# Rows of logits that go through memory in the expert stages k = 2 to 7, and two products a tile for the tokens' numbers where k is odd

## The chip, the core and the metric

The kernel is one program on one core of a Trainium2 chip. The core has a matrix engine (TensorE: PE in the profile, its weight loads PEld), a vector engine (VectorE, DVE), an activation engine (ScalarE, ACT), GpSimd (POOL) and SyncE (SP); each takes its instructions in a fixed order and waits on semaphores. POOL and SP issue DMAs, POOL the indirect ones (gathers and scatters). The metric is the device time of one execution in microseconds (us), the median of several.

## The reference

Three parts follow one another, cut here to what matters:

```python
# 1. retention with decay, blocks of 64: q, k, v are (2, 8, 768, 64); x is (1536, 512)
x = attn_out.transpose(0, 2, 1, 3).reshape(1536, 512)
# 2. tokens to 8 experts, 192 tokens each, greedily by falling logit
logits = x @ w_gate
for idx in np.argsort(-logits.flatten()):
    tok, e = idx // 8, idx % 8
    if assigned[tok] >= 0 or counts[e] >= 192: continue
    assigned[tok] = e; counts[e] += 1
for e in range(8):
    out[assigned == e] = np.maximum(x[assigned == e] @ w1[e], 0) @ w2[e]   # 512 -> 1024 -> 512
# 3. a dense layer on every token: 512 -> 2048 -> 512, ELU between
g = elu(out @ w_in);  result = g @ w_out
```

## The kernel before

The retention comes first (the first 95 us), and it leaves the logits and the tokens' rows `xd` in memory. Then come eight stages k = 0 to 7. The greedy assignment is done expert by expert: the expert that fills first, its 192 tokens, then the expert that fills first among those left, and so on. `R.n` is the number of tiles of 128 tokens still listed: 12 for k = 0 and 1, 9 for k = 2 and 3, 6 for 4 and 5, 3 for 6 and 7. Before each even stage from k = 2 on `pack(k)` drops the assigned tokens: one scatter per tile from POOL (L710) into `open`, then one fetch (`new`, L723).

For a stage k the steps of routing are, in this order:

- `update(k)`. `close` (L739 to L742) shuts the filled expert and leaves each token's best open logit in `m` (128 partitions, one column per tile). `rows_` (L760) transposes on PE, for each tile, that tile's column spread over 128 columns, so that PSUM holds the 128 logits as a row on every partition; ACT copies up to four such tiles at once into `mrow` (L763). Then `cmp` compares on DVE for each tile c the whole of `mrow` with column c of `m` (L425, L421, L428), and `tally` (L783) sums the outcome on PE, n small products a tile. The result is each token's rank.
- `choose(k)`. `theta`, `close`, `mine` find the next expert to fill, its number (`EV`, read by SP for the weights' loads) and its tokens; `index` (L877) makes the 192 tokens' numbers by products of a one-hot matrix `ohs` with `mt`, one product per tile and column. One product gives 128 slots, so an even stage has two columns (slots 0 to 127 and 128 to 191), an odd stage three: slots 64 to 191, 0 to 63 on partitions 0 to 63, and 0 to 63 again on partitions 64 to 127. The third serves only `ixm`, the list by which the middle output tile of a pair of stages is sent. `gb` and `ga` (L896, L902) gather the rows of `xd` into `xb` and `xa`.
- `x_parts(k)` transposes `xb` and `xa` (L943) and splits the result into `xt`; `weights(k)` loads w1 and w2 and, for k > 1, splits them on ACT and DVE (`w1p`, `w2p`: L1011, L1014).

The stage's own work on PE is h (`xt`, `w1p`), y (`ht`, `w2p`), g (`yt`, `wih`/`wil`) and, by pairs of stages, the output products (`gg`, `woh`/`wol`). Numbers with more than 16 bits are taken as a sum of two 16-bit parts, three products each. The routing of stage k + 1 is worked in beside g of stage k and what follows it.

All steps are handed to a planner (`Plan`) as tasks with an engine, a cost, dependencies, a lag, and a bonus `ahead`; it orders them by its own costs and writes one fixed order for each engine. POOL's scatters of `pack` also wait for the PE instruction that stands ahead of them in that order. So a changed task moves others on all engines.

Of the kernel before, what the change touches and what calls it, by code (L numbers as in the profile page):

```python
# [19 lines left out]
FT = mybir.dt.float32  # L20
# [3 lines left out]
AF = mybir.ActivationFunctionType  # L24
# [14 lines left out]
AHEAD, XAHEAD, WAHEAD, EAHEAD, GLAG, APART = 15.0, 4.0, 5.0, 3.0, 3.5, 1.2  # L39
# [7 lines left out]
class Plan:  # L47
# [10 lines left out]
    def add(self, eng, cost, fn, *deps, lag=0.0, ahead=0.0, look=0.15, mode=None):  # L58


        t = dict(eng=eng, cost=cost, fn=fn, lag=lag, ahead=ahead, look=look, mode=mode, n=len(self.tasks))
        t["deps"] = [d if isinstance(d, tuple) else (d, 0.0) for d in deps if d is not None]
        self.tasks.append(t)
        return t
# [38 lines left out]
def kernel(  # L103
# [13 lines left out]
    nc = tc.nc  # L117
    B, H, S, D = q.shape
    C = 128
    NC = S // C  # L120
    NT = B * NC
# [5 lines left out]
    CAP = N // E  # L127
# [5 lines left out]
    route = ctx.enter_context(tc.tile_pool(name="route", bufs=1))  # L133
    dram = ctx.enter_context(tc.tile_pool(name="dram", bufs=1, space=bass.MemoryType.DRAM))
    psum = ctx.enter_context(tc.tile_pool(name="psum", bufs=1, space=bass.MemoryType.PSUM))

    def bank(tag, bufs=1):
        return psum.tile([128, 512], FT, name="ps_" + tag, tag=tag, bufs=bufs)
# [25 lines left out]
    identf = consts.tile([128, 128], FT)  # L164
# [31 lines left out]
    for i, (r0, o) in enumerate(((0, 0), (0, 64), (64, 0))):  # L196
# [3 lines left out]
                                  ap=[[E, step], [256 * E, HP // 2], [1, E]]))  # L200
# [60 lines left out]
    xd = dram.tile([N, DM], FT)  # L261
# [119 lines left out]
    class R:  # L381
        n = NT
# [4 lines left out]
    m = route.tile([128, NT], FT, name="m")  # L387
# [9 lines left out]
    mrow = route.tile([128, N], FT, name="mrow")  # L397
# [65 lines left out]
    add = hp.add  # L463
# [82 lines left out]
    while at < len(pairs):  # L546
        n = max(pairs[at])
# [12 lines left out]
    use, use2 = [None, None], [None, None]  # L560
# [53 lines left out]
    add = pl.add  # L614
# [14 lines left out]
    RB_ = ("m", "o")  # L629
# [36 lines left out]
    EV, ev_task = {}, {}  # L666
    wst = {}
    rk = route.tile([128, NT], FT, name="rk")
    th = route.tile([128, 2, E], FT, name="th")
    mt = route.tile([128, NT], HF, name="mt")  # L670

# [60 lines left out]
    def update(k):  # L732

        n, L, act, ws = R.n, R.L, R.act, wst[0]
        sh = [128, n, E]
        t = tp_[:, 0:n, :]

        def close():
            nc.vector.tensor_scalar(cl, e8, ws, None, op0=OP.is_equal)  # L739
            nc.vector.tensor_scalar(cl, cl, -2.0 * BIG, BIG, op0=OP.mult, op1=OP.add)  # L740
            nc.vector.tensor_tensor(L, L, cl[:, None, :].to_broadcast(sh), op=OP.min)
            nc.vector.tensor_reduce(m[:, 0:n], L, axis=AX, op=OP.max)  # L742

        def top():
            nc.vector.tensor_tensor(t, L, m[:, 0:n, None].to_broadcast(sh), op=OP.is_equal)
            nc.vector.tensor_tensor(t, t, e8b.to_broadcast(sh), op=OP.mult)
            nc.vector.tensor_reduce(wv[:, 0:n], t, axis=AX, op=OP.max)
            nc.vector.tensor_tensor(t, wv[:, 0:n, None].to_broadcast(sh), e8b.to_broadcast(sh), op=OP.is_equal)
            nc.vector.tensor_tensor(oh[:, 0:n, :], t, act[:, :, None].to_broadcast(sh), op=OP.mult)
        d = add("DVE", 0.95, close, R.task, last_compare[0])  # L750
        row = []
        for b in range(0, n, 4):
            e = min(n, b + 4)
            i, old, use = rbank.take()
            S = {}

            def rows_(b=b, e=e, i=i, S=S):
                S["p"] = p = bank(RB_[i])
                for c in range(b, e):
                    nc.tensor.transpose(p[:, (c - b) * 128:(c - b + 1) * 128], m[:, c:c + 1].to_broadcast([128, 128]), identf)  # L760
            r = add("PE", 0.11 * (e - b), rows_, (d, 0.3), *old, ahead=AHEAD)
            r = add("ACT", 0.3 + 0.08 * (e - b),
                    lambda b=b, e=e, S=S: nc.scalar.activation(mrow[:, b * 128:e * 128], S["p"][:, 0:(e - b) * 128], AF.Copy),  # L763
                    r, last_compare[0], ahead=AHEAD)
            use.append(r)
            row.append(r)
        d = add("DVE", 1.2, top, d)

        ci, old, cuse = rbank.take()

        def cmp(c, j):
            o = gts[j]
            if c:
                below(o[:, 0:128 * c], c, 0, c)
            tie(o[:, 128 * c:128 * c + 128], c)
            if c < n - 1:
                upto(o[:, 128 * c + 128:128 * n], c, c + 1, n)

        def tally(c, j):
            if c == 0:  # L780
                cnt[0] = bank(RB_[ci])
            for t in range(n):
                nc.tensor.matmul(cnt[0][:, E * t:E * t + E], gts[j][:, 128 * t:128 * t + 128], oh[:, c, :],  # L783
                                 start=c == 0 and t == 0, stop=c == n - 1, skip_group_check=True)
        pc = None
        for c in range(n):
            j, gold, guse = gtr.take()
            cost = 0.31 + 0.16 * (1 if c in (0, n - 1) else 2) + 0.00052 * 128 * (n - 1)
            d = add("DVE", cost, lambda c=c, j=j: cmp(c, j), d, *row, *gold)
            pc = add("PE", 0.027 * n, lambda c=c, j=j: tally(c, j), (d, 0.6), pc, *old, ahead=AHEAD)  # L790
            guse.append(pc)
        last_compare[0] = d
        return pc, cuse

    def choose(k, pc, cuse):
# [71 lines left out]
        i, old, use = rbank.take()  # L867
        T = {}

        js = ((0, 128), (64, 0, -64))[k % 2]  # L870

        def index(j):
            if j == 1:
# [4 lines left out]
                                 stop=c == n - 1, skip_group_check=True)  # L878
        got = {}
        p = None  # L880
        for j in (1, 0, 2)[0:len(js)]:
            p = add("PE", 0.027 * n, lambda j=j: index(j), (d, 0.3), p, *fills, *(old if j == 1 else ()), ahead=AHEAD)
            got[j] = add("DVE", 0.16, lambda j=j: nc.vector.tensor_copy(idx[:, k, j:j + 1], T["p"][:, j:j + 1]), (p, 0.2),  # L883
                         ahead=AHEAD, look=look)
            use.append(got[j])
# [4 lines left out]
        if k % 2:  # L890

            def middle():
                nc.vector.tensor_copy(ixm[0:64, k // 2:k // 2 + 1], idx[0:64, k - 1, 1:2])
                nc.vector.tensor_copy(ixm[64:128, k // 2:k // 2 + 1], idx[64:128, k, 2:3])
            add("DVE", 0.3, middle, got[2])
        gb = add("POOL", 1.05, lambda: nc.gpsimd.indirect_dma_start(  # L896
            out=xb[0:64], out_offset=None, in_=xd, in_offset=bass.IndirectOffsetOnAxis(ap=idx[0:64, k, 1:2], axis=0)),
            got[1], *xa_free[0], lag=GLAG, ahead=2 * AHEAD)
        GA = {}

# [21 lines left out]
    x_ready, w1_ready, w2_ready = {}, {}, {}  # L922

    def x_parts(k, gb, ga):
        ca, cb = ((0, 128), (64, 0))[k % 2]
        whole = k in WHOLE
        tr, out_ = [], []
        for g in range(2):
            if k == 0:
                i, old, use = (xbank, rbank)[g].take()  # L930
                tag = ("x", RB_[i])[g]
            else:
                i, old, use = xbank.take()
                tag = "x"
            S = {}


            def turn(src, at, g=g, S=S, tag=tag):
                if "p" not in S:
                    S["p"] = bank(tag)  # L940
                for i in range(2):
                    r = 2 * g + i
                    nc.tensor.transpose(S["p"][:, i * CAP + at:i * CAP + at + 128], src[:, r * 128:(r + 1) * 128], identf)  # L943
            t = add("PE", 0.22, lambda turn=turn: turn(xb, cb), gb, *old, ahead=XAHEAD)
            t = add("PE", 0.22, lambda turn=turn: turn(xa, ca), ga, t, ahead=XAHEAD)
            tr.append(t)
            sl = slice(2 * g, 2 * g + 2)

            def hi(S=S, sl=sl, g=g):
                pv = S["p"][:, 0:2 * CAP].rearrange("p (a n) -> p a n", a=2)  # L950
                if whole:
                    (nc.vector.tensor_copy if g else nc.scalar.copy)(
                        xt.rearrange("p a r n -> p (a r n)").bitcast(FT).rearrange("p (r n) -> p r n", r=RD)[:, sl, :], pv)
                else:
                    nc.scalar.activation(xt[:, 0, sl, :], pv, AF.Copy, scale=SX)
            a = add("DVE" if whole and g else "ACT", 0.5, hi, t, h_done.get(k - 1), ahead=XAHEAD)
            if not whole:
                def lo(S=S, sl=sl):
                    pv = S["p"][:, 0:2 * CAP].rearrange("p (a n) -> p a n", a=2)
                    nc.vector.scalar_tensor_tensor(xt[:, 1, sl, :], pv, SX, xt[:, 0, sl, :], op0=OP.mult, op1=OP.subtract)  # L960
                a = add("DVE", 0.53, lo, a, ahead=XAHEAD)
            use.append(a)
            out_.append(a)
        xa_free[0] = tr
        x_ready[k] = out_
# [328 lines left out]
```

## Time and profile before

| what | value |
|---|---|
| median of 3 runs | 540.31 us (539.79 to 542.95) |
| profiled execution, its own time | 538.41 us |
| its span, first to last instruction | 536.6 us |
| PE busy | 508.5 us |
| DVE, ACT, POOL busy | 360.3, 307.5, 93.2 us |
| mean granted clock of TensorE | 0.976 |

The profile is of one execution, so its numbers are added up against 538.41 us, which lies 1.9 us under the median. Times of rows are microseconds from the start of the span.

### The profile page before, as it was taken

Reading aid. Unit: us, or ns where it says so; the run is one execution under the profiler, and the core shown is the slowest. Engines: PE = TensorE matmul, PEld = TensorE weight load, DVE = VectorE, ACT = ScalarE, POOL = GpSimd, SP = SyncE. Lnnn points to the kernel's source line nnn. Section 1 sums busy time; section 2 is a strip of 40 time slices with the busy share of each in tenths; the row PEclk is TensorE's granted clock in tenths of the full one; section 3 lists DMA queues with packets and bytes.
Section 4 is the critical chain, followed back from the end, with each engine's and each line's share of the span. In section 5 each row is a group of like instructions: output and inputs, shape, how many; then the busy total and the mean of one; then the engine's idle time right before and its main releaser. Section 6 shows DMA issues by size and latency. Waiting matters only on the chain.

```text
span 536.6 us, 12988 instructions
## 1 busy us (share of the span) xinstructions
PE 508.5 (95%) x5362; PEld 426.4 (79%) x5362; DVE 360.3 (67%) x807; ACT 307.5 (57%) x646; POOL 93.2 (17%) x124
## 2 busy tenths in 40 slices
PE   4999898799999899999999999999999999999994
PEld 4888777789899874589969955996898489879941
DVE  3499999997999698387587675747557653671410
ACT  2768754423893575454982795468449533961910
POOL 1231240200335101030451101012401001000000
PEclk8799998699999999999999999999999999999999
DMA  6999935286594204250440225052205505040000
GB/s 121 246 246 272 301 102 207 73 312 279 180 325 167 79 2 155 73 176 6 185 162 25 104 89 173 21 189 77 105 3 187 177 21 187 1 177 1 2 21 20
DMA packets 62762, 70.43 MB, mean 131 GB/s; under 512 B 40704, under 2 KB 45264, under 8 KB 61680
## 3 DMA queue, kind: packets, MB, share of 16 engines
q1 hardware_dynamic: 58496, 62.92, 36.7%
q0 software_dynamic: 2960, 6.66, 3.7%
q8 instruction: 42, 0.69, 0.5%
q10 hardware_dynamic: 1248, 0.02, 0.1%
q14 instruction: 16, 0.13, 0.1%
HBM read 63.08 MB, written 6.51 MB: 130 GB/s over the span
## 4 chain that ended last, share of the span: by engine, by line
PE 66%; DVE 15%; issue 6%; DMA 5%; ACT 5%; POOL 1%; POOLq 0%; ACTq 0%; DVEq 0%
PE ps_t L1022 5%; PE ps_s L1023 5%; PE ps_t L1023 5%; PE ps_s L1022 5%; PE ps_s L1024 5%; PE ps_t L1024 5%; PE ps_s L1192 3%; PE ps_s L1190 3%; PE ps_s L1191 3%; PE ps_S L1022 2%; PE ps_S L1023 2%; PE ps_S L1024 2%; PE ps_t L1190 2%; PE ps_t L1192 2%; PE ps_t L1191 2%
## 5 line engine op out<-in xcount | busy, mean ns | idle before, releaser
L1023 PE MATMUL ps_t<-yt,wih 128*128 128x192 f16 x208 | 51.2, 246 | 0.8 <-DVE yt L1109 0.8
L1024 PE MATMUL ps_t<-yt,wil 128*128 128x192 f16 x208 | 51.2, 246 | 0.0
L1022 PE MATMUL ps_t<-yt,wih 128*128 128x192 f16 x208 | 51.1, 246 | 0.0
L1024 PEld LDWEIGHTS <-wil 128*128 128x128 f16 x512 | 50.1, 98 | 1.0 <-issue 0.9
L1022 PEld LDWEIGHTS <-wih 128*128 128x128 f16 x512 | 50.3, 98 | 0.0
L1023 PEld LDWEIGHTS <-wih 128*128 128x128 f16 x512 | 50.0, 98 | 0.2
L1024 PE MATMUL ps_s<-yt,wil 128*128 128x192 f16 x200 | 49.2, 246 | 0.0
L1023 PE MATMUL ps_s<-yt,wih 128*128 128x192 f16 x200 | 49.2, 246 | 0.0
L1022 PE MATMUL ps_s<-yt,wih 128*128 128x192 f16 x200 | 49.2, 246 | 0.0
L710 POOL DMA_INDIRECT open<-rec,dest x27 | 32.6, 1206 | 51.1 <-DVE dest L699 18.3
L1192 PEld LDWEIGHTS <-gg 128*128 128x128 f16 x192 | 18.8, 98 | 23.4 <-DVE gg L1171 0.9
L1192 PE MATMUL ps_s<-woh,gg 128*128 128x512 f16 x96 | 36.4, 379 | 0.4 <-DVE gg L1171 0.4
L1191 PE MATMUL ps_s<-wol,gg 128*128 128x512 f16 x96 | 36.4, 379 | 0.0
L1190 PE MATMUL ps_s<-woh,gg 128*128 128x512 f16 x96 | 36.4, 379 | 0.0
L1171 DVE TENSOR_TENSOR gg<-el,gg 128x384 f16<-128x384 f32 x64 | 34.3, 552 | 1.7 <-ACT gg L1170 1.6
L1163 ACT ACTIVATE el<-el 128x384 f32<-128x384 f32 x64 | 33.4, 522 | 1.9
L1164 ACT ACTIVATE el<-el 128x384 f32<-128x384 f32 x64 | 33.4, 521 | 1.8
L1191 PEld LDWEIGHTS <-gg 128*128 128x128 f16 x192 | 18.8, 98 | 19.4
L1014 DVE SCALAR_TENSOR_TENSOR w2p<-stg,w2p 128x1024 f16<-128x1024 f32 x24 | 28.3, 1220 | 8.7 <-ACT w2p L1011 8.7
L1190 PEld LDWEIGHTS <-gg 128*128 128x128 f16 x192 | 18.8, 98 | 19.2
L1170 ACT ACTIVATE gg<-el 128x384 f16<-128x384 f32 x64 | 31.2, 509 | 2.3 <-DVE el L1165 2.3
L902 POOL DMA_INDIRECT xa<-xd,idx x8 | 9.4, 1177 | 130.9 <-DVE idx L883 130.2
(265 smaller groups left out, 1578.7 us busy)
## 6 DMA issues: line engine op xcount, KB each, us to landing
stg<-in_moe_w_dram SPq DMA_DIRECT2D x24, 1024.0 KB, 5.7
stg<-in_moe_w_in_dram SPq DMA_DIRECT2D x7, 1024.0 KB, 6.1
stg<-in_moe_w_out_dram SPq DMA_DIRECT2D x6, 1024.0 KB, 5.5
w1p<-in_moe_w_dram SPq DMA_DIRECT2D x8, 512.0 KB, 4.5
w2p<-in_moe_w_dram SPq DMA_DIRECT2D x8, 512.0 KB, 8.3
kn<-in_k_dram SPq DMA_DIRECT2D x12, 256.0 KB, 4.5
qn<-in_q_dram SPq DMA_DIRECT2D x12, 256.0 KB, 5.3
vn<-in_v_dram SPq DMA_DIRECT2D x12, 256.0 KB, 4.7
```

The costliest lines, as they stand in the source:

```text
L710: st = nc.gpsimd.indirect_dma_start(out=buf, out_offset=bass.IndirectOffsetOnAxis(ap=dest[:, c:c + 1], axis=0), in_=rec[:, c, :], in_offse ...
L1014: nc.vector.scalar_tensor_tensor(part(1), T["t"][:, 1024 * z:1024 * z + 1024], sc, part(0), op0=OP.mult, op1=OP.subtract)
L1022: nc.tensor.matmul(o, wh, xh, start=first, stop=False, skip_group_check=True)
L1023: nc.tensor.matmul(o, wh, xl, start=False, stop=False, skip_group_check=True)
L1024: nc.tensor.matmul(o, wl, xh, start=False, stop=last, skip_group_check=True)
L1163: a = add("ACT", 0.49, lambda: nc.scalar.activation(e_, e_, AF.Exp, scale=-1.0), a, ahead=EAHEAD)
L1164: a = add("ACT", 0.49, lambda: nc.scalar.activation(e_, e_, AF.Copy, scale=SG, bias=-SG), a, ahead=EAHEAD)
L1170: a = add("ACT", 0.49, lambda: nc.scalar.activation(gh, two(e_), AF.Copy), a, *free, ahead=EAHEAD)
L1171: a = add("DVE", 0.53, lambda: nc.vector.tensor_tensor(gl, two(e_), gh, op=OP.subtract), a, ahead=EAHEAD)
L1190: nc.tensor.matmul(p, GH[:, f, c], woh[:, f, :], start=f == 0, stop=False, skip_group_check=True)
L1191: nc.tensor.matmul(p, GH[:, f, c], wol[:, f, :], start=False, stop=False, skip_group_check=True)
L1192: nc.tensor.matmul(p, GL[:, f, c], woh[:, f, :], start=False, stop=f == RF2 - 1, skip_group_check=True)
```

## The change

Two edits, and what the planner makes of them.

First, for k > 1 `rows_` is gone. PE transposes all n columns of `m` at once into n rows of 128 (`turned`), ACT copies these n rows into `mcol` (16 partitions), POOL writes `mcol` to a buffer `md` in memory, and a second DMA of POOL reads `md` back with a step of zero over the partitions, so that all 128 partitions of `mrow` get the n rows. The stages k = 0 and 1 keep their rows on PE.

Second, where k is odd `index` makes two columns: slots 64 to 191, and slots 0 to 63 on partitions 64 to 127, which serve both `ixm` and the gather of `xb`. That gather now takes 128 partitions, of which the first 64 fetch token 0, and the transposed tokens start at column 64 of the PSUM bank (`z0`).

```diff
         d = add("DVE", 0.95, close, R.task, last_compare[0])
         row = []
-        for b in range(0, n, 4):
+        if k > 1:
+            i, old, use = rbank.take()
+            S = {}
+            def turned(i=i, S=S):
+                S["p"] = bank(RB_[i])
+                nc.tensor.transpose(S["p"][0:n, 0:128], m[:, 0:n], identf)
+            md = dram.tile([NT, 128], FT, name=f"md{k}")
+            r = add("PE", 0.11, turned, (d, 0.3), *old, ahead=AHEAD)
+            r = add("ACT", 0.2, lambda S=S: nc.scalar.activation(mcol[0:n, :], S["p"][0:n, 0:128], AF.Copy), r, row_read[0],
+                    ahead=AHEAD)
+            use.append(r)
+            r = add("POOL", 0.92, lambda: nc.gpsimd.dma_start(md[0:n, :], mcol[0:n, :]), r, lag=2.0, ahead=AHEAD)
+            row_read[0] = r
+            r = add("POOL", 0.92, lambda: nc.gpsimd.dma_start(mrow[:, 0:n * 128], bass.AP(
+                tensor=md.tensor, offset=md.offset, ap=[[0, 128], [1, n * 128]])), r, last_compare[0], lag=3.5, ahead=AHEAD)
+            row.append(r)
+        for b in range(0, n if k == 1 else 0, 4):
...
-        js = ((0, 128), (64, 0, -64))[k % 2]
+        js = ((0, 128), (64, -64))[k % 2]
+        half = slice(0, 128 if k % 2 else 64)
...
-        for j in (1, 0, 2)[0:len(js)]:
+        for j in (1, 0):
...
-                nc.vector.tensor_copy(ixm[64:128, k // 2:k // 2 + 1], idx[64:128, k, 2:3])
+                nc.vector.tensor_copy(ixm[64:128, k // 2:k // 2 + 1], idx[64:128, k, 1:2])
...
-            out=xb[0:64], out_offset=None, in_=xd, in_offset=bass.IndirectOffsetOnAxis(ap=idx[0:64, k, 1:2], axis=0)),
+            out=xb[half], out_offset=None, in_=xd, in_offset=bass.IndirectOffsetOnAxis(ap=idx[half, k, 1:2], axis=0)),
...
-        ca, cb = ((0, 128), (64, 0))[k % 2]
+        ca, cb = ((0, 128), (128, 0))[k % 2]
+        z0 = 64 * (k % 2)
```

Lines after L749 of the kernel before stand 19 to 21 lines lower in the changed one (L1014 is L1035, L1055 L1076, L1095 L1116, L1022 to L1024 L1043 to L1045).

What the planner makes of it is shown at three places. The first is PE where y of stage 1 (L1095, L1116: 32 products into two banks) ends and g of stage 1 begins. Before:

```order
L1055 MATMUL ps_t_2302<-xt,w1p 128x192 x8
L1055 MATMUL ps_s_2317<-xt,w1p 128x192 x8
L1095 MATMUL ps_S<-ht,w2p 128x192 x16
L1095 MATMUL ps_t_2362<-ht,w2p 128x192 x16
L1022 LDWEIGHTS wih
L1022 MATMUL ps_s_2390<-yt_1445,wih 128x192
L1023 LDWEIGHTS wih
```

Now:

```order
L1076 MATMUL ps_s_2315<-xt,w1p 128x192 x8
L1116 MATMUL ps_S<-ht,w2p 128x192 x16
L1116 MATMUL ps_t_2359<-ht,w2p 128x192 x16
L760 MATMUL ps_m<-identf,m 9x128
L1043 LDWEIGHTS wih
L1043 MATMUL ps_s_2396<-yt_1445,wih 128x192
```

The transposition of stage 2's best logits (L760) stands ahead of all of g of stage 1; the nine of before stood behind its first 72 products. The last scatter of `pack(2)` moved too: it stood behind the 24th of y's 32 products and now stands behind the 8th.

The second is DVE in the same stretch, from y's first evacuation (`yt` from ps_S) on. Before, the second `yt` came ahead of the fetched tokens (`L<-new`):

```order
L1109 SCALAR_TENSOR_TENSOR yt_1445<-ps_S,yt_1445 128x384
L249 SCALAR_TENSOR_TENSOR f_119<-stg_116,f_119 128x1024
L252 SCALAR_TENSOR_TENSOR wol<-f_118,woh 128x1024
L252 SCALAR_TENSOR_TENSOR wol<-f_119,woh 128x1024
L1109 SCALAR_TENSOR_TENSOR yt_1445<-ps_t_2362,yt_1445 128x384
L243 TENSOR_SCALAR f_118<-stg_117 128x1024
L246 SCALAR_TENSOR_TENSOR f_118<-stg_117,f_118 128x1024
L727 COPY L_1436<-new 128x72
```

Now the fetched tokens come first, `close` (L740 to L743) and `top` (L746 to L750) follow, and the second `yt` stands behind them and a split of `wol`; from the last row of `close` on:

```order
L743 TENSOR_REDUCE m<-L_1436 128x9
L746 TENSOR_TENSOR tp<-L_1436,m 128x72
L747 TENSOR_TENSOR tp<-tp,e_85 128x72
L748 TENSOR_REDUCE wv<-tp 128x9
L749 TENSOR_TENSOR tp<-wv,e_85 128x72
L750 TENSOR_TENSOR oh<-tp,act_1438 128x72
L252 SCALAR_TENSOR_TENSOR wol<-f_118,woh 128x1024
L1130 SCALAR_TENSOR_TENSOR yt_1445<-ps_t_2359,yt_1445 128x384
```

All of this, from `L<-new` to `oh`, is moved ahead of the second `yt`, and g's second half waits for that `yt`.

The third is DVE ahead of h of stage 2, where the tokens (`xt`), the split w1 (`w1p`, four rows of w1 in two pairs) and the compares of stage 3 (`gt`) meet. Before:

```order
L960 SCALAR_TENSOR_TENSOR xt<-ps_x,xt 128x384
L1014 SCALAR_TENSOR_TENSOR w1p<-stg_117,w1p 128x1024 x2
L960 SCALAR_TENSOR_TENSOR xt<-ps_x,xt 128x384
L421 SCALAR_TENSOR_TENSOR gt_1448<-mrow,m,before 128x128
L428 TENSOR_SCALAR gt_1448<-mrow,m 128x1024
L1014 SCALAR_TENSOR_TENSOR w1p<-stg_116,w1p 128x1024 x2
```

Now:

```order
L981 SCALAR_TENSOR_TENSOR xt<-ps_x,xt 128x384 x2
L421 SCALAR_TENSOR_TENSOR gt_1448<-mrow,m,before 128x128
L428 TENSOR_SCALAR gt_1448<-mrow,m 128x1024
L1035 SCALAR_TENSOR_TENSOR w1p<-stg_117,w1p 128x1024 x2
L425 TENSOR_SCALAR gt_1449<-mrow,m 128x128
L421 SCALAR_TENSOR_TENSOR gt_1449<-mrow,m,before 128x128
L428 TENSOR_SCALAR gt_1449<-mrow,m 128x896
L1035 SCALAR_TENSOR_TENSOR w1p<-stg_116,w1p 128x1024 x2
```

The first pair of `w1p` is moved behind both halves of `xt` and behind the first compare, the second pair behind two compares.

## Rows read from the trace of the kernel before

**Rows 1.** The page's first part: engines' busy time, share, instructions.

```profile
PE 508.5 (95%) x5362; PEld 426.4 (79%) x5362; DVE 360.3 (67%) x807; ACT 307.5 (57%) x646; POOL 93.2 (17%) x124
```

**Rows 2.** The windows: stretch, length, each engine's busy time, clock, DMA.

```profile
300.00:320.00 20.00, 20.00 (x190) 15.41 (x189) 13.40 (x39) 19.52 (x42) 2.00 (x3) 1.00 0.34 125
```

**Rows 3.** PE's waits: line, releaser, total us, times, longest us.

```profile
PE ps_m L760 <- DVE m L742: 1.8, 1, 1.8
PE ps_s L1192 <- DVE gg L1171: 0.4, 1, 0.4
```

**Rows 4.** Line L760, PE's transposes: count, duration ns, first and last start.

```profile
L760 PE MATMUL ps_m<-identf,m x26: 272/273/323, 109.5 to 436.9; 128*128 128x128 f32 x26
L760 PE MATMUL ps_o<-identf,m x22: 272/273/421, 102.5 to 333.7; 128*128 128x128 f32 x22
```

**Rows 5.** The chain that ended last: start, length, what.

```profile
173.41 5.12 DMA open<-rec,dest
...
287.95 0.44 PE ps_o L760 x4
```

**Rows 6.** PE in order of time: start, length, line, operation.

```profile
175.56 0.25 PE L1022 MATMUL ps_s<-yt,wih 128*128 128x192 f16 x1
...
220.36 0.38 PE L943 MATMUL ps_x<-identf,xb 128*128 128x128 f32 x2
...
224.04 0.38 PE L943 MATMUL ps_x<-identf,xa 128*128 128x128 f32 x2
...
230.22 0.24 PE L1022 MATMUL ps_t<-xt,w1p 128*128 128x192 f16 x1
...
256.47 0.59 PE L877 MATMUL ps_o<-mt,ohs 128*128 128x1 f16 x18
256.93 0.24 PE L1022 MATMUL ps_s<-yt,wih 128*128 128x192 f16 x1
...
287.29 0.25 PE L1022 MATMUL ps_s<-ht,w2p 128*128 128x192 f16 x1
...
287.54 0.25 PE L1022 MATMUL ps_s<-ht,w2p 128*128 128x192 f16 x1
```

**Rows 7.** POOL in order of time, two of pack(2)'s scatters, the gather after them.

```profile
168.21 1.90 POOL L710 DMA_INDIRECT open<-rec,dest  x1 [1.54 <-PE ps_S L1095]
...
173.41 1.35 POOL L710 DMA_INDIRECT open<-rec,dest  x1 [1.34 <-PE ps_t L1095]
...
214.30 0.93 POOL L896 DMA_INDIRECT xb<-xd,idx  x1 [0.30 <-issue]
```

**Rows 8.** DVE in order of time, from stage 2's best logits to stage 4's.

```profile
183.21 0.23 DVE L742 TENSOR_REDUCE m<-L 128x9 f32<-128x72 f32 x1
...
225.04 0.56 DVE L960 SCALAR_TENSOR_TENSOR xt<-ps_x,xt 128x384 f16<-128x384 f32 x1 [0.21 <-ACT xt L955]
...
227.56 2.36 DVE L1014 SCALAR_TENSOR_TENSOR w1p<-stg,w1p 128x1024 f16<-128x1024 f32 x2 [0.19 <-ACT w1p L1011]
229.84 0.28 DVE L425 TENSOR_SCALAR gt<-mrow,m 128x128 f16<-128x128 f32 x1
...
230.89 0.35 DVE L425 TENSOR_SCALAR gt<-mrow,m 128x256 f16<-128x256 f32 x1
...
295.40 0.56 DVE L1109 SCALAR_TENSOR_TENSOR yt<-ps_t,yt 128x384 f16<-128x384 f32 x1 [0.64 <-ACT yt L1105]
```

**Rows 9.** DMA issues: tile, count, KB each, median us to landing.

```profile
stg<-in_moe_w_dram SPq DMA_DIRECT2D x24, 1024.0 KB, 5.7
...
open<-rec,dest POOLq DMA_INDIRECT x27, 3.7
...
xa<-xd,idx POOLq DMA_INDIRECT x8, 5.3
...
new<-open POOLq DMA_DIRECT2D x1, 72.0 KB, 3.1
...
new<-open POOLq DMA_DIRECT2D x1, 48.0 KB, 2.7
```

More of the change, by code (lines that the diff above doesn't have):

```diff
@@ L668 @@
     rk = route.tile([128, NT], FT, name="rk")
+    mcol, row_read = route.tile([16, 128], FT, name="mcol"), [None]
     th = route.tile([128, 2, E], FT, name="th")
@@ L893, in middle @@
                 nc.vector.tensor_copy(ixm[0:64, k // 2:k // 2 + 1], idx[0:64, k - 1, 1:2])
-                nc.vector.tensor_copy(ixm[64:128, k // 2:k // 2 + 1], idx[64:128, k, 2:3])
-            add("DVE", 0.3, middle, got[2])
+                nc.vector.tensor_copy(ixm[64:128, k // 2:k // 2 + 1], idx[64:128, k, 1:2])
+            add("DVE", 0.3, middle, got[1])
         gb = add("POOL", 1.05, lambda: nc.gpsimd.indirect_dma_start(
-            out=xb[0:64], out_offset=None, in_=xd, in_offset=bass.IndirectOffsetOnAxis(ap=idx[0:64, k, 1:2], axis=0)),
+            out=xb[half], out_offset=None, in_=xd, in_offset=bass.IndirectOffsetOnAxis(ap=idx[half, k, 1:2], axis=0)),
             got[1], *xa_free[0], lag=GLAG, ahead=2 * AHEAD)
@@ L949, in hi @@
             def hi(S=S, sl=sl, g=g):
-                pv = S["p"][:, 0:2 * CAP].rearrange("p (a n) -> p a n", a=2)
+                pv = S["p"][:, z0:z0 + 2 * CAP].rearrange("p (a n) -> p a n", a=2)
                 if whole:
@@ L958, in lo @@
                 def lo(S=S, sl=sl):
-                    pv = S["p"][:, 0:2 * CAP].rearrange("p (a n) -> p a n", a=2)
+                    pv = S["p"][:, z0:z0 + 2 * CAP].rearrange("p (a n) -> p a n", a=2)
                     nc.vector.scalar_tensor_tensor(xt[:, 1, sl, :], pv, SX, xt[:, 0, sl, :], op0=OP.mult, op1=OP.subtract)
```

## The prediction

> **What bounds the kernel now.** The page's first part comes first: PE is busy for 95% of the span, DVE for 67%, ACT for 57% [rows 1]. The windows say where the other 5% lie: in the stages from 188 us on a stretch of 20 us holds 20.00 us of PE [rows 2], so PE's idle time is in the retention and the first stages. Of its waits in the part that the change touches only two are left, 1.8 us on `m` of stage 2 and 0.4 us on `gg` [rows 3]. So a PE instruction taken away from stages 2 to 7 is worth its own length, and a wait put there costs its whole length. Work taken from ACT, DVE or POOL is worth nothing by itself. The profiled execution took 538.41 us; I add to that and then 1.9 us for the median.
>
> **What PE loses.** Line L760 holds 48 transposes [rows 4]: 12 of k = 1, 36 of k = 2 to 7 (9 + 9 + 6 + 6 + 3 + 3), which become 6. Four take 0.44 us on the chain [rows 5], one 0.11. The duration of 0.27 that the line shows is a pipelined length, not what PE is held for. 30 x 0.11 = **3.3 us**. The index products go from three to two per tile for k = 1, 3, 5, 7, with 12, 9, 6 and 3 tiles: 30 fewer. Eighteen of them hold PE from 256.47 to 256.93 [rows 6], 0.0256 each: **0.8 us**. Sum −4.1 us. Fewer ACT copies of `mrow` and one `idx` copy less on DVE lie on engines with room; I count them at nothing. The gather of `xb` takes 128 rows in place of 64 where k is odd; `xa` with its 128 takes 5.3 us (a median over all stages) [rows 9]. What covers it is the output products between gather and transposes; if the cover is gone it costs a few tenths in four stages, which the range holds.
>
> **A new wait ahead of g of stage 1.** The transposition of `m` now stands ahead of all of g instead of behind 72 products. Before, PE was done with y at 175.56 [rows 6], did 72 products of g and then waited 1.8 us for `m` [rows 3], which came at 183.21 + 0.23 [rows 8]. `m` comes from the last scatter of `pack(2)`, issued at 173.41 [rows 7] and 5.12 us long in the chain [rows 5]: 10.0 us from scatter to `m`. In the new order that scatter follows the 8th product of y, about where one of before was issued at 168.21 [rows 7]: 5.2 us earlier, so `m` comes at 178.2. PE, at y's end at 175.56, waits 2.7 us in place of 1.8; with a scatter of the median 3.7 us [rows 9] it would be 1.3. All of g is queued behind this wait. The second `yt` has moved behind `m`, five short steps of `top` (about m's 0.23 each, 1.2 us), a split of `wol` (a pair of splits of this size goes from 227.56 to 229.84, so 1.14) and itself (0.56 in the row at 295.40, of which I count 0.5, as rows of DVE overlap a little [rows 8]): 2.8 us after `m`. PE has 24 products of g's first half for it; three such products take 287.54 − 287.29 = 0.25 us [rows 6], so 2.0 us. A second wait of 0.8. The net price is 2.7 + 0.8 − 1.8 = 1.7, with the shorter scatter 0.3. I take **+1.5**, near the row that this very scatter has.
>
> **A new wait ahead of h of stage 2.** Its first product came at 230.22 [rows 6], and the last pair of `w1p` was done at 229.84 [rows 8], when the compares began: no slack was left. Now both pairs stand behind compares. DVE's second `xt` starts at 225.04 and has ended at about 225.5 [rows 8]; four transposes of `m` that stood ahead of its source are gone, so 225.1. Then a compare of one tile (229.84 to 230.89, 1.05 us [rows 8]), a pair of `w1p` (2.28), a compare, a pair: 6.7 us, to 231.7. PE is there at 230.22, less nine transposes (1.0), plus the third index product below (0.2): 229.5. If all of w1 is needed for the first products it waits 2.2 us, if the first pair does for a while about 0.5. I take **+1.3**, between them, since h goes through the rows of w1 in turn. The output products and the tally behind it give no cover: PE's order is fixed.
>
> **What is not gained.** One of the four removed columns (k = 3, 9 products, 0.23 us) stands ahead of the wait of 0.4 on `gg` [rows 3], which takes it back: **+0.2**.
>
> **The way through memory.** Transposition and copy take about 0.4 us (0.11 and an ACT step that I put at 0.3, by the DVE steps of this size in rows 8). A write from POOL has no row of its kind; the nearest are the fetches of 48 and 72 KB with 2.7 and 3.1, and the scatters with a median of 3.7 and one of 5.12 [rows 5, 9]. The read of 590 KB has as neighbours a gather of 128 rows with 5.3, a load of 1 MB with 5.7, and below it the fetch with 2.7 [rows 9]. So the pair takes 5.4 to 11.2 us; I take 3.1 + 4.5 + 0.4 = **8 us**, with the read nearer to the gather. What hides it: for k = 2, g of stage 1 and a DVE that is full of splits. For k = 3 the transposition stands 18 output products ahead of the x transposes at 220.36. Between 220.36 and 224.04 lie 12 such products and ten transposes [rows 6], so one takes (3.68 − 1.1)/12 = 0.215; the transposition is at 216.5 and the rows arrive at 224.5, or somewhat later behind the two gathers issued up to 214.30 + 0.93 [rows 7]. They are wanted at 225.1: no slack to speak of. DVE stands in order behind this compare with both pairs of `w1p`, and PE's h behind these. For k = 4 the transposition is at 287.95 [rows 5]; 72 products of y and 48 of g stand ahead of the first tally, 120 x 0.083 = 9.9 us, of which a compare takes 0.9: about 1 us of slack. I put the same for k = 5, 6 and 7.
>
> For the read the rows say 5.3 for a 256 KB gather and 3.1 for a 72 KB fetch [rows 9]. The Trainium skill ("DMA: Bandwidth & Descriptors", section "Anatomy of one DMA — SWDGE (gpsimd) path") has a fit for a DMA from GpSimd, 2.0 us plus bytes over 436 KB per us, which would be 2.6 and 2.2 for these two; the trace has them longer, so I do not go by it. By it the pair would be an estimated 2.2 + 3.4 + 0.4 = 6.0 us, with slack everywhere: the sum would stay, and the slow rival below would fall away.
>
> **Sum.** −4.1 + 1.5 + 1.3 + 0.2 = −1.1, so 537.3 for a profiled execution and **539.2 us** against the median.
>
> **Rivals.**
> A, the forecast: the two new waits eat three quarters of the gain. With both ends of each wait it spans −4.1 + 0.3 + 0.5 + 0.2 = −3.1 to −4.1 + 1.7 + 2.2 + 0.2 = 0.
>
> B, the cover holds: the waits come out at their lower ends or under them. Speaks for it that scatters usually take 3.7, and that h needs one row of w1 at a time. −3.1, 537.2.
>
> C, slower: rows late. In every stage from k = 3 DVE stands behind the first compare, and behind DVE stand `w1p`, the tally and PE. Each us beyond 8 costs one at k = 3; at four more stages what is over 9. Slower than before begins at a pair of 9.1 us. At 10.2 us it is 2.2 + 4 x 1.2 − 1.1 = +5.9, over 1%. At 10.5, 2.5 + 4 x 1.5 − 1.1 = +7.4: 547.7. For it: the weights' loads of 1 MB share the DMA engines, one scatter took 5.12, and the read waits for the write to land. Against it: no median of a single DMA is over 5.7 [rows 9].
>
> D, the waits vanish as well as the work, the old 1.8 included: −4.1 − 1.8 = −5.9, 534.4, faster by 1.1%. Against it: `m` would have to come 2.7 us earlier than its scatter allows.
>
> That the change would not do what it says is ruled out by the new order, which shows 6 transposes where 36 stood.
>
> **How the numbers follow.** A 0.52, B 0.21, C 0.22, D 0.05. 1% (5.4 us) is about what a measurement of this kernel can tell from no change. A, B and the mild end of C, pairs of 9.1 to 10.2 us, to which I give 0.06 of its 0.22, lie inside it: same 0.79, faster 0.05, slower 0.16. The range goes from B's 537.2, less 1 us for waits that vanish altogether, to a pair of 9.9 us (1.9 + 4 x 0.9 − 1.1 = +4.4, 544.7) and a little on, since the pair has no row of its own: 536.2 to 545.5.
>
> **What would show it.** In the profile after: 18 executions of L760, each stage from k = 2 with one; PE waiting for `m` at the start of g of stage 1 by about 2.7 us and for `yt` by 0.8; PE waiting for `w1p` (L1035) at the first products of h of stage 2; the read of `md` landing about 8 us after the transposition, and DVE waiting for `mrow` in no stage but k = 3, and there under 1 us. PE's busy time should fall by about 4 us (to 504), less what idle time it swaps for. Were PE idle behind a compare that waits for the DMA in several stages, C is right; were both new waits under half a us, B. The forecast is wrong most easily in the length of the pair, which no row shows, and in any PE wait of the later stages that I did not look for in the new order.

## The result, and the profile after

The changed kernel takes 545.88 us (545.14 to 546.71, six runs), the kernel before 539.5 us (538.6 to 542.95, six runs): a ratio of 1.0113, with a 95% interval of 1.0091 to 1.0135. It is slower by 1.1%. The forecast was 539.2 us with a range that ended at 545.5.

The profiled execution has a span of 543.97 us against 536.64, 7.3 us more. Where they arise is read from the starts of the same blocks of PE's work in both traces (first product of h, y, g or of the output products of a stage):

| stretch | ends before at | ends after at | it adds |
|---|---|---|---|
| to h of stage 0 | 109.99 | 110.94 | +0.95 |
| to g of stage 1 | 175.56 | 180.34 | +3.83 |
| g of stage 1 | 195.34 | 198.51 | −1.61 |
| to g of stage 2 | 249.16 | 253.40 | +1.07 |
| to y of stage 4 | 342.51 | 345.38 | −1.37 |
| to y of stage 5 | 386.24 | 390.45 | +1.34 |
| y of stage 5 | 394.73 | 401.37 | +2.43 |
| to the last product | 528.75 | 535.10 | −0.29 |
| to the end of the span | 536.64 | 543.97 | +0.98 |

The first row is no effect of the change: it arises in the retention and the first routing, and in the runs below with the same order it lies between −0.44 and +0.95. The two large rows are two places.

First the page's first part and the line of the transpositions, which answer to [rows 1, 4]:

```profile
PE 507.4 (93%) x5302; PEld 424.5 (78%) x5302; DVE 359.6 (66%) x803; ACT 303.8 (56%) x640; POOL 102.3 (19%) x136
```

```profile
L760 PE MATMUL ps_m<-identf,m x4: 272/272/277, 180.2 to 436.8; 128*9 128x128 f32 x2, 128*3 128x128 f32 x2
L760 PE MATMUL ps_o<-identf,m x2: 272/272/273, 291.9 to 330.3; 128*6 128x128 f32 x2
```

The change does what it says: six transpositions at this line (the twelve of k = 1 stand at L779 now, so the 18 that were forecast for L760 are split over two lines), 60 PE instructions fewer. But PE's share fell from 95% to 93%: it has less work and idles more. Its busy time fell by 1.1 us and not by the 4 that were forecast; 1.7 us of the difference are work at half speed, shown below. Its waits (line, releaser, total, times, longest), which answer to [rows 3]:

```profile
PE ps_m L760 <- DVE m L743: 3.9, 1, 3.9
PE ps_t L1044 <- DVE ht L1091: 3.3, 3, 1.6
...
PE ps_s L1044 <- DVE ht L1091: 1.7, 2, 1.4
...
PE ps_t L1045 <- DVE w1p L1035: 0.7, 1, 0.7
...
PE ps_s L1213 <- DVE gg L1192: 0.7, 1, 0.7
```

The wait on `m` is the first place, the waits on `ht` are mostly the second. At the first, the windows (stretch, length, busy time of each engine, clock, DMA share and rate) show more than the wait:

```profile
176.00:180.00 4.00, 0.29 (x2) 0.00 (x0) 0.91 (x7) 0.00 (x0) 0.00 (x0) 1.00 0.47 184
...
181.00:182.00 1.00, 1.00 (x10) 0.95 (x8) 0.96 (x3) 0.18 (x1) 0.60 (x1) 0.50 0.07 16
182.00:183.00 1.00, 1.00 (x8) 0.95 (x7) 1.00 (x2) 0.00 (x0) 0.00 (x0) 0.50 0.03 5
183.00:184.00 1.00, 1.00 (x8) 0.95 (x7) 1.00 (x2) 0.00 (x0) 0.29 (x1) 0.50 0.00 0
184.00:185.00 1.00, 1.00 (x12) 0.98 (x11) 0.96 (x3) 0.00 (x0) 0.30 (x1) 0.79 0.00 0
```

After 3.94 us of idling PE ran at a granted clock of 0.50, its level of 1.2 GHz, for three of these windows and 0.42 us of the fourth: 3.4 us at half speed, 1.7 us of work lost. The chain of waits has the two DMAs behind the wait, to be read beside 5.12 for the scatter in [rows 5] and 3.1 for the 72 KB fetch in [rows 9]:

```profile
168.77 5.56 DMA open<-rec,dest
...
174.92 4.04 DMA new<-open
```

The second place, DVE in order of time between h and y of stage 5:

```profile
387.01 0.18 DVE L728 COPY L<-new 128x24 f32<-128x24 f32 x1 [6.73 <-DMA new<-open]
...
387.96 2.35 DVE L1035 SCALAR_TENSOR_TENSOR w2p<-stg,w2p 128x1024 f16<-128x1024 f32 x2
...
391.19 0.55 DVE L1091 SCALAR_TENSOR_TENSOR ht<-ps_s,ht 128x384 f16<-128x384 f32 x1
391.66 2.35 DVE L1035 SCALAR_TENSOR_TENSOR w2p<-stg,w2p 128x1024 f16<-128x1024 f32 x2
393.93 0.55 DVE L1091 SCALAR_TENSOR_TENSOR ht<-ps_S,ht 128x384 f16<-128x384 f32 x1
```

and PE waiting for these two `ht`:

```profile
391.79 0.24 PE L1044 MATMUL ps_t<-ht,w2p 128*128 128x192 f16 x1 [1.10 <-DVE ht L1091]
...
394.53 0.24 PE L1044 MATMUL ps_t<-ht,w2p 128*128 128x192 f16 x1 [1.58 <-DVE ht L1091]
```

In the new order DVE's copy of the tokens that `pack(6)` fetches stands ahead of both pairs of `w2p` and of all `ht` of stage 5. DVE stood 6.73 us behind that fetch, and so behind the scatters ahead of it, with them queued. In the kernel before the copy stood behind the last `ht`, and the same kind of wait cost PE nothing, as these rows of DVE show:

```profile
386.96 0.56 DVE L1070 SCALAR_TENSOR_TENSOR ht<-ps_s,ht 128x384 f16<-128x384 f32 x1 [1.42 <-ACT ht L1066]
391.81 0.18 DVE L727 COPY L<-new 128x24 f32<-128x24 f32 x1 [4.29 <-DMA new<-open]
```

Last the DMAs of the rows (tile, count, KB, median us to landing), which answer to [rows 9], and for two stages the issue of write and read on POOL and the first compare on DVE:

```profile
mrow<-md POOLq DMA_DIRECT2D x2, 576.0 KB, 4.1
...
mrow<-md POOLq DMA_DIRECT2D x2, 384.0 KB, 5.5
open<-rec,dest POOLq DMA_INDIRECT x27, 5.4
...
md<-mcol POOLq DMA_DIRECT2D x2, 4.5 KB, 2.3
```

```profile
292.76 0.57 POOL L766 DMA_DIRECT2D md<-mcol  x1 [5.72 <-ACT mcol L763]
294.94 0.59 POOL L768 DMA_DIRECT2D mrow<-md  x1 [1.61 <-DMA md<-mcol]
```

```profile
300.44 0.35 DVE L421 SCALAR_TENSOR_TENSOR gt<-mrow,m,before 128x128 f16<-128x128 f32 x1 [0.77 <-DMA mrow<-md]
339.39 0.35 DVE L421 SCALAR_TENSOR_TENSOR gt<-mrow,m,before 128x128 f16<-128x128 f32 x1 [3.23 <-DMA mrow<-md]
```

The transposition of k = 4 began at 291.9 and the rows were there at 300.4: 8.5 us; for k = 5 it is 330.3 to 339.4, 9.1 us. DVE waited for rows in these two stages only, 0.77 and 3.23, or 4.0 us in all.

Two theories follow. **Order**: the change made the planner put steps of routing ahead of work that was ready, while the scatters and the fetch that they need were still under way; PE pays at g of stage 1 and y of stage 5. **Late rows** (rival C): the pair of DMAs is too long, DVE stands behind `mrow`, and `ht` follows late.

### The profile page after: what moved, and what is told of

It reads as the page before. It is cut to its first block, busy times and chain, and to the rows that moved or that the text cites. A ratio compares the mean times of both kernels' runs of the same rounds, so it can differ in the third digit from the quotient of the medians.

```text
span 544.0 us, 12877 instructions
## 1 busy us (share of the span) xinstructions
PE 507.4 (93%) x5302; PEld 424.5 (78%) x5302; DVE 359.6 (66%) x803; ACT 303.8 (56%) x640; POOL 102.3 (19%) x136
## 4 chain that ended last, share of the span: by engine, by line
PE 57%; issue 16%; DVE 14%; DMA 7%; ACT 3%; POOL 1%; POOLq 0%; ACTq 0%; DVEq 0%
PE ps_s L1044 4%; PE ps_s L1043 4%; PE ps_s L1045 4%; PE ps_t L1044 3%; PE ps_t L1045 3%; PE ps_t L1043 3%; DMA stg<-in_moe_w_dram 3%; PE ps_s L1211 2%; PE ps_s L1212 2%; PE ps_s L1213 2%; PE ps_t L1211 2%; PE ps_t L1213 2%; PE ps_t L1212 2%; PE ps_s L1076 2%; DMA open<-rec,dest 2%
## 5 line engine op out<-in xcount | busy, mean ns | idle before, releaser
L1045 PE MATMUL ps_t<-yt,wil 128*128 128x192 f16 x208 | 51.6, 248 | 0.0
L1043 PE MATMUL ps_t<-yt,wih 128*128 128x192 f16 x208 | 51.6, 248 | 0.0
L1045 PEld LDWEIGHTS <-wil 128*128 128x128 f16 x512 | 50.4, 98 | 0.9 <-issue 0.8
L1043 PEld LDWEIGHTS <-wih 128*128 128x128 f16 x512 | 50.8, 99 | 0.1
L1045 PE MATMUL ps_s<-yt,wil 128*128 128x192 f16 x200 | 49.6, 248 | 0.0
L1043 PE MATMUL ps_s<-yt,wih 128*128 128x192 f16 x200 | 49.5, 248 | 0.0
L1035 DVE SCALAR_TENSOR_TENSOR w2p<-stg,w2p 128x1024 f16<-128x1024 f32 x24 | 28.4, 1220 | 7.1 <-ACT w2p L1032 7.1
L1032 ACT ACTIVATE w2p<-stg 128x1024 f16<-128x1024 f32 x24 | 24.1, 1048 | 12.0 <-DMA stg<-in_moe_w_dram 12.0
```

Of the source, the lines that this page charges most:

```text
L1035: nc.vector.scalar_tensor_tensor(part(1), T["t"][:, 1024 * z:1024 * z + 1024], sc, part(0), op0=OP.mult, op1=OP.subtract)
L1043: nc.tensor.matmul(o, wh, xh, start=first, stop=False, skip_group_check=True)
L1045: nc.tensor.matmul(o, wl, xh, start=False, stop=last, skip_group_check=True)
```

## The experiments

All ratios are to the kernel before, run on the same chip as the run itself. The runs below were made on three chips, on which the kernel before took 539.3, 541.3 and 539.3 us, so they are compared by their ratios.

**Index products alone.** The rows stay on PE in all stages:

```diff
-        if k > 1:
...
-        for b in range(0, n if k == 1 else 0, 4):
+        for b in range(0, n, 4):
```

> Only the index products are changed; the rows of logits stay on PE in all stages. Order theory (the new order puts routing steps ahead of work that the chip could do, while the scatters and the fetch they need are still under way): the order hardly differs from before, so no wait of over 2 us on m before g of stage 1 and none on ht in y of stages 2 and 5; 0.8 us faster than before, about 538.7. Late-rows theory (the rows that go through memory arrive too late and hold up DVE): no row goes through memory, so also about 538.7. Index theory (the wider gather and the shared slots cost the time): slower than before by several us, 542 or more.

Measured: 539.9 us, ratio 1.0017 (0.9993 to 1.004). No slowdown, so the wider gather and the shared slots are not its cause, and no gain of 0.8 us either. The chain has the last scatter of stage 2's tokens at

```profile
173.54 6.47 DMA open<-rec,dest
```

where it took 5.12 before [rows 5], issued at the same point of PE's order; the wait on `m` grew from 1.83 to 3.20 us and ate the gain.

**Rows alone.** The odd stages keep three products.

```diff
-        js = ((0, 128), (64, -64))[k % 2]
+        js = ((0, 128), (64, 0, -64))[k % 2]
```

> Only the rows are changed; an odd stage keeps three index products. In its order the transposition of stage 2 stands ahead of g of stage 1 as in the full change, but the fetched tokens of stage 6 stand on DVE behind three of the four ht of stage 5. Order theory: the wait before g of stage 1 (about 3.9 us) stays, the two waits of y of stage 5 on ht (2.7 us) go, 0.8 us of products come back: 545.9 - 2.7 + 0.8 = 544.0. Late-rows theory: the same pairs of DMAs, so nothing but the 0.8 us: 546.7.

Measured: 543.65 us, 1.0081 (1.0052 to 1.011). PE waits 4.01 us on `m` and nothing on `ht` in y of stage 5, though 2.54 on `ht` in y of stage 2, where it is 1.42 in the change. The DMA pairs are those of the change, and without the moved copy of stage 6 the time is lower, near the order theory's 544.0.

**The order of the change, rows on PE.** The planner gets the tasks of the change, so that the order is kept, but PE makes the rows (`four` transposes up to four columns, each spread over 128, as `rows_` did) and no pair of DMAs is issued:

```diff
-                nc.tensor.transpose(S["p"][0:n, 0:128], m[:, 0:n], identf)
+                four(S["p"], 0)
+                if n > 4:
+                    S["q"] = bank(RB_[1 - i])
+                    four(S["q"], 4)
...
-            r = add("POOL", 0.92, lambda: nc.gpsimd.dma_start(md[0:n, :], mcol[0:n, :]), r, lag=2.0, ahead=AHEAD)
+            r = add("POOL", 0.92, lambda: None, r, lag=2.0, ahead=AHEAD)
```

> The order of the full change on every engine, but the rows are made on PE and copied by ACT, with no DMA pair: the first eight columns where the one transposition stood, the ninth where the read stood. Order theory: all new waits (m before g of stage 1, ht in y of stages 2 and 5) stay, and PE has 30 transposes more: 545.9 + 3.3 = 549.2. Late-rows theory: DVE no longer waits for mrow, the ht follow earlier, PE loses only the wait on m: 545.9 + 3.3 - 5 = 544.

Measured: 549.17 us, 1.0169 (1.0136 to 1.0202), the order theory's 549.2. PE's waits in it:

```profile
PE ps_m L760 <- DVE m L743: 4.6, 1, 4.6
PE ps_s L1063 <- DVE ht L1110: 2.2, 1, 2.2
...
PE ps_t L1063 <- DVE ht L1110: 1.6, 1, 1.6
```

With no row late, the waits on `m`, on `ht` in y of stage 2 and the larger one of stage 5 are there. Three shorter ones on `ht` (0.28, 0.61 and 1.10 us in the change) are gone; whether by the rows or because PE comes later was not tried. So most of the loss is the order's. That the sum came out to 0.1 us is in part luck: besides 30 transpositions more and these 2.0 us less, the waits on `m` and in y of stage 2 are 0.7 and 0.8 us longer, the end of the span is 1.0 us shorter, and behind the 2.2 us in y of stage 2 the clock fell a second time, for 3.4 us, where it stays at 1.00 in the change:

```profile
251.00:252.00 1.00, 1.00 (x9) 0.94 (x8) 1.00 (x3) 0.00 (x0) 0.00 (x0) 0.50 0.06 16
```

**Stage 2's rows on PE.** In the planner's order for this, the first place is as it was before.

```diff
-        if k > 1:
+        if k > 2:
...
-        for b in range(0, n if k == 1 else 0, 4):
+        for b in range(0, n if k < 3 else 0, 4):
```

> The full change, but the rows of stage 2 stay on PE; in its order nine transposes again stand behind 72 products of g of stage 1, the second yt ahead of the fetched tokens. Order theory: the place before g of stage 1 comes back to what it was (its net price was about 2.6 us with the low clock after it), the wait of y of stage 5 stays: 545.9 - 2.6 = 543.3. Late-rows theory: the pair of stage 2 was hidden anyway, so at most the wait on m changes into 0.9 us of transposes, and the ht waits of stages 2 and 5 stay: 545 to 546.5.

Measured: 541.73 us, 1.0044 (1.0015 to 1.0073), 0.7% under the change, where the order theory had 0.5% and the late-rows theory at most 0.2%. It is not the price of the first place alone. There PE still waits 3.18 us on `m`, but the clock stays at 1.00 behind it; and in stage 2 the wait on `w1p` (0.71) is gone, and that on `ht` is 0.42 in place of 1.42. The waits on `ht` in y of stage 5 stay (0.81 and 1.58 us).

**Stage 6's fetch placed later, and both.** The planner counts 4.0 us from the fetch's issue to its landing; here 11.0 for stage 6, so that the copy comes behind three `ht`.

```diff
-                    p, lag=4.0, ahead=AHEAD)
+                    p, lag=4.0 if k < 6 else 11.0, ahead=AHEAD)
```

> The full change, with only the planner's figure for the fetch of stage 6 raised from 4.0 to 11.0 us, so that DVE's copy of the fetched tokens comes behind three ht of stage 5; the rows of stage 2 go through memory as in the change. Order theory: the two waits of y of stage 5 on ht (1.10 + 1.58 us) go and nothing else: ratio to before 1.0113 - 2.7/540 = 1.006, some 543. Late-rows theory: 1.011 or more.

> As the run with the rows of stage 2 on PE, and the planner is told that the fetch of stage 6 takes 11.0 us in place of 4.0, so that DVE's copy of the fetched tokens comes behind three of the four ht of stage 5 and no longer ahead of the split w2 and of all ht. Order theory: the two waits of y of stage 5 on ht (0.81 + 1.58 us) go: 541.7 - 2.4 = 539.3. Late-rows theory: the pairs of DMAs are the same, 541.7, or more, since stage 6 starts later.

Measured: 542.23 us, 1.0053 (1.0033 to 1.0072) for this alone; 538.72 us, 0.9959 (0.9931 to 0.9988), with stage 2's rows on PE as well. In neither does PE wait for `ht` in y of stage 5. From the change's 1.0113 the rows of stage 2 on PE give back 0.7%, the later fetch 0.6%, both together 1.5%: they about add up, and with both the slowdown is gone, though five of the six pairs are still issued.

**Busy in the wait.** 14 products ahead of stage 2's transposition:

```diff
+                for _ in range(14 if k == 2 else 0):
+                    nc.tensor.matmul(S["p"][:, 0:128], onesf, onesf, start=True, stop=True)
```

> The full change with 14 products of ones ahead of stage 2's transposition, which PE does while it waits for m. They are no part of the reference's work and their sum is overwritten. Clock theory: after the wait of 3.94 us the granted clock stood at 0.50 for 3.4 us, which is 1.7 us of work lost; with PE busy in the wait it stays at 1.00: 545.9 - 1.7 = 544.2. If the low clock only covered time in which PE would have waited for yt anyway: 545.9.

Measured: 547.11 us, 1.011 (1.0078 to 1.0142): no gain. Behind the wait on `m` the granted clock stayed at 1.00, but in this run the fetch issued at 175.46 came late:

```profile
181.00 0.23 DVE L728 COPY L<-new 128x72 f32<-128x72 f32 x1 [7.12 <-DMA new<-open]
```

That is 5.5 us against 4.1 in the change, and behind the faster products PE waited 0.60 us for the second `yt`, which the low clock had hidden. So the clock's share was there to be had (g of stage 1 and what follows up to the output products shortened by 2.5 us against the kernel before, by 1.6 in the change), and the later `m` took 1.5 us. Further on, in y of stage 2, PE waited longer for `ht` than in the change (1.42), and behind it the clock fell after all:

```profile
248.22 0.24 PE L1046 MATMUL ps_s<-ht,w2p 128*128 128x192 f16 x1 [2.64 <-DVE ht L1093]
251.00:252.00 1.00, 1.00 (x9) 0.95 (x7) 1.00 (x4) 0.00 (x0) 0.00 (x0) 0.50 0.00 0
```

From y to g of stage 2 that cost 2.9 us more than in the change. As a test of the low clock's price in the whole time the run is inconclusive.

**Each read twice.**

```diff
+                for _ in range(2):
+                    nc.gpsimd.dma_start(mrow[:, 0:n * 128], bass.AP(
...
```

> The full change, in which each read of md into mrow is issued twice, one behind the other, so that the pair is longer by one read (3.8 to 5.5 us), say 4.5. Late-rows theory as the prediction priced it (each us costs one at k = 3, and at four more stages what is over 1 us): 4.5 + 4 x 3.5 = 18 us, 564. Order theory: the rows were late by 0.8 us at k = 4 and 3.2 us at k = 5 with little loss on PE, so part of it stays covered by DVE's own slack: some 3 to 9 us, 549 to 555.

Measured: 557.31 us, 1.0321 (1.0279 to 1.0362), some 11 us more than the change by the ratios, between the two theories' sums, for a second read of 3.6 to 5.7 us. DVE's waits on rows rose from 4.0 to

```profile
DVE gt L421 <- DMA mrow<-md: 19.0, 5, 9.1
```

and PE now stood behind the tally of stages 3, 4 and 5 (up to 3.2 us at once); behind the waits of stages 3 and 5 the clock fell to 0.50 for 3.4 us each, which is another 3.4 us of work lost. Late rows do cost what rival C said in kind; in the change itself they were not late enough.

**Idle pairs beside the kernel before.** A constant tile is written and copied 128 times in memory; the rows stay on PE.

```diff
+            nc.gpsimd.dma_start(md[0:n, :], identf[0:n, :])
+            nc.gpsimd.dma_start(md2, bass.AP(tensor=md.tensor, offset=md.offset, ap=[[0, 128], [1, n * 128]]))
...
```

> The kernel before, in which POOL also writes a constant tile to a buffer in memory and copies it 128 times to another buffer in memory, for k = 2 to 7, at the time of the rows; nothing waits for it but POOL. The order of PE and DVE is that of before. In the runs so far the time from the last product to the end is 8.7 to 8.9 us with such pairs and 7.9 without: if that is their own cost, 539.3 + 0.9 = 540.2, and the rest of the time is as before. If the pairs also disturb scatters and gathers, the wait on m before g of stage 1 grows and it is 541 to 542.

Measured: 540.72 us, 0.9997 (0.9972 to 1.0023). The wait on `m` of stage 2 is 1.88 us, as before; the only new wait behind the pairs is one of 0.72 us on `m` of stage 6. The interval holds both no change and the 0.9 us that were expected, so the whole time decides nothing here. The end of the span in the trace does; it is told of below.

**A load held back.** In the kernel before the last 1 MB load of `w_out` is in flight beside the last scatter of `pack(2)`: it is issued at 172.80 and lands at 178.35, the scatter is issued at 173.41 and lands at 178.53.

```profile
172.80 0.37 SPq L215 DMA_DIRECT2D stg<-in_moe_w_out_dram  x1
```

Here that load waits for the fetch; the orders of PE, ACT and DVE stay.

```diff
+                    tc.add_manual_dep(st, FETCH[0].ins.name, AFTER, reason="the open tokens are needed first")
...
```

> The kernel before, in which SP's last 1 MB load of w_out waits until the tokens of stage 2 have been fetched; every engine's order is that of before. Load theory (the last scatter of stage 2's tokens and the fetch are long because that load shares the DMA engines with them): scatter 5.1 to about 3.7 us, so the wait on m of 1.8 us falls to about 0.3: ratio 0.997. If scatter and fetch take what they take by themselves: 1.000, or more where the late load is missed.

> The full change with the same load held back; the order is that of the full change. Load theory: scatter 5.6 to 3.7 and fetch 4.0 to 3.1 us, the wait on m 3.9 to about 1.2, the clock stays at 1.00 (1.7 us), the second yt is waited for by 0.6: 2.7 + 1.7 - 0.6 = 3.8 us less, ratio 1.0113 - 0.007 = 1.004. If the two DMAs take what they take by themselves: 1.011.

> The run with stage 2's rows on PE and stage 6's fetch placed later (ratio 0.996), with the same load held back. Load theory: scatter 6.8 to about 3.7 us, the wait on m 3.5 to about 0.4, the clock stays at 1.00 behind it (1.7 us): 3.1 + 1.7 = 4.8 us less, ratio 0.987. If the scatter takes what it takes by itself: 0.996.

Measured: the kernel before with it 537.21 us, 0.9958 (0.9937 to 0.9978), with a scatter of 2.54 us, a fetch of 3.54 and no wait on `m` of stage 2 left, as the load theory had it; the change with it 544.76 us, 1.0093 (1.0063 to 1.0122); the repaired change with it 537.13 us, 0.9954 (0.9937 to 0.9971). In the last, scatter and fetch took

```profile
173.81 4.70 DMA open<-rec,dest
179.10 3.13 DMA new<-open
```

against 6.76 and 3.16 without, and the wait on `m` fell from 3.52 to

```profile
183.50 0.32 PE L793 MATMUL ps_m<-identf,m 128*128 128x128 f32 x1 [1.43 <-DVE m L757]
```

In the other two the load theory missed. In the change only the fetch got shorter (4.0 to 3.1) and the wait on `m` went from 3.94 to 3.01; the scatter kept its 5.55 us, which lies in the time of the load before that one, and the clock fell as before. The ratio is 0.2% lower where 0.7% was expected, within the noise. The repaired change was to go from 0.9959 to 0.987; it stayed at 0.9954, though the wait on `m` is shorter by 2.1 us and the clock stays at 1.00 behind it. So that load is part of the length of these DMAs, not all of it, and what the shorter waits are worth in the whole time is shown for the kernel before alone.

## Why the prediction was wrong

**The steps that held.** PE loses the transpositions and products as counted: added up from start to start in the two traces, 36 transpositions hold PE for 4.0 us before and six for 0.7 after, the index products for 4.0 and 3.3, which is 4.1 us together. The pair of DMAs was put at 8 us and took 7.6 for k = 2 and 8.5 and 9.1 for k = 4 and 5, transposition and copy included. The Trainium skill's fit ("DMA: Bandwidth & Descriptors", section "Anatomy of one DMA — SWDGE (gpsimd) path") gave an estimated 6.0 (5.8 if the write is taken by its own 4.5 KB), so the measurement decides against it here. The wait on `gg` grew from 0.41 to 0.67, the 0.2 that it was to take back. The wait ahead of h of stage 2 came, on `w1p` as forecast, but with 0.71 in place of 1.3; the 1.0 more on `ht` in y of that stage was in no step.

**"A new wait ahead of g of stage 1", +1.5.** The mechanism was right, the term too small. The wait was 3.94, not 2.7: on the clock of before `m` came at 179.6, not 178.2, since the moved scatter took 5.56 for 5.12 and the fetch 4.04 for 3.1. I moved the chain forward with the lengths that it had where it stood. At its new place the fetch lay beside a 1 MB load, and with that load held back it took 3.1 again; why the scatter was longer stays open, since it lay beside such a load at both places. And the price ended with the wait: the 1.7 us at the low clock behind it were not in the sum, while the 0.8 for the second `yt` did not come, hidden by that low clock. 3.94 + 1.7 − 1.83 is 3.8 in place of 1.5.

**"Any PE wait of the later stages that I did not look for in the new order."** The prediction named this as a way to be wrong. This is the term that was missing, put at nothing: y of stage 5 with 1.10 + 1.58 us, and 0.28 and 0.61 on `ht` of stages 3 and 4, 3.6 us in all. I read the new order at three places, all of stages 1 to 3. The copy of stage 6's tokens had moved past `w2p` and `ht` in the same way as that of stage 2 had moved past `yt`, and was not looked for.

**The end of the span.** Another 1.0 us that no step of the prediction had; the last section tells what it goes with.

With these the sum is −4.1 + 3.8 (stage 1) + 1.7 (stage 2, 0.71 + 1.0) + 0.3 (the longer wait on `gg`) + 3.6 (stages 3 to 5) + 1.0 = +6.3, beside 6.4 between the profiled executions (7.33 less the 0.95 of the first row of the table). Its terms are read from this one trace, so it is bookkeeping; the tests are the runs above.

**Rival C** gave a number close to the result (547.7), by luck. Of its chain, DVE did stand behind rows for 4.0 us, at k = 4 and 5 and not at k = 3, and the doubled read shows what that costs when it grows; but with no rows to wait for the loss stayed, and with the fetch of stage 6 placed later and all six pairs still issued half of it went. Its slack was also wrong by stage: with a second read of 3.6 to 5.7 us, k = 5 lost most, k = 6 and 7 little. Rival B needed the scatter's usual 3.7 us, which this scatter had in none of the chains shown.

**Where the expected gain went.** The repaired change, with the load held, equals the kernel before with the load held (0.9954 and 0.9958). It leaves out 22 transpositions and 30 products, 3.2 us, and gives them back: 1.43 us on `m`, 0.8 at the end, and the rest in waits longer by 0.2 to 0.3 on `yt`, `ht` and `gg`. Why the last scatter takes 4.70 us there and 2.54 in the kernel before with the load held is not settled; its issue has the same place in PE's order.

## What to carry to other kernels

When one planner orders everything, a step that gets a longer tail can be pulled ahead in many stages, here at g of stage 1 and y of stage 5, and an engine that takes its instructions in order then stands behind a DMA that used to be hidden. Read the new order at every stage in which the moved step stands, ask at each what is queued behind its wait, and take a DMA's length at the place where it will stand and not where it stood. Raising the planner's figure for one fetch from 4.0 to 11.0 us, so that what waits for it is placed later (the fetch itself took 2.6), gave back 0.6%, or 3.2 us, beside the 4.1 us of work that the whole edit takes off PE.

## What the runs showed of the hardware

A wait of PE can cost more than itself: behind 3.94 us of idling the granted clock was 0.50 for 3.4 us, behind 3.52 us (stage 2's rows on PE, stage 6 later) it was

```profile
186.00:187.00 1.00, 1.00 (x7) 0.92 (x6) 0.90 (x5) 0.79 (x2) 0.00 (x0) 0.50 0.00 0
```

and behind 3.20 us (index products alone) it stayed at 1.00:

```profile
185.00:189.00 4.00, 4.00 (x45) 3.98 (x46) 3.86 (x11) 2.94 (x7) 0.00 (x0) 1.00 0.00 0
```

The length of the wait alone does not decide it. The clock also fell behind 3.01 us (the change with the load held), 2.64 (busy in the wait, y of stage 2) and 2.21 (the order kept, y of stage 2), and it stayed at 1.00 behind 3.18 (stage 2's rows on PE) and 2.54 (rows alone, y of stage 2).

From the last product's start to the end of the span the time goes with the number of DMAs that POOL issues:

| runs | POOL's instructions on the page | last product to the end, us |
|---|---|---|
| before, index products alone, order kept with rows on PE, before with the load held | 124 | 7.88 to 7.89 |
| stage 2's rows on PE (three runs) | 134 | 8.70 to 8.71 |
| the change, rows alone, busy in the wait, stage 6 later, load held; before with idle pairs | 136 | 8.87 |
| each read twice | 142 | 9.36 |

That is 0.08 us for each DMA of POOL that is added, 10, 12 or 18 of them, and the idle pairs, whose data nothing uses, bring as much as the others. So the six pairs bring 1.0 us at the end merely by being in the program. By which mechanism was not tried.
